# A last output quarter copied by two engines with one store moved to GpSimd, and V scaled first in four retention steps

## The chip, the cores and the metric

The kernel runs on one core of a Trainium2 chip. The metric is the time of one execution on the device in microseconds (us); where several runs are given, the median counts. The core's engines are TensorE (PE, matrix products; PEld is its loading of weights), VectorE (DVE), ScalarE (ACT), GpSimd (POOL) and SyncE (SP). Each runs its own list of instructions in order and waits on semaphores for what others produce. SyncE, ScalarE and GpSimd can issue DMA transfers; an engine that issues one is occupied while it does so.

## The reference

Retention (an attention without softmax, with a decay per head) over 8 sequences of 576 tokens, 8 heads of 64, followed by a two-layer network with hard-swish:

```python
scores = scale * np.matmul(q, k.transpose(0, 1, 3, 2))
gamma = 1.0 - 2.0 ** (-5.0 - np.arange(H, dtype=np.float32))
rel = pos[:, None] - pos[None, :]
Dmat = np.where(rel >= 0, gamma[:, None, None] ** rel[None, :, :], 0.0)
x = np.matmul(scores * Dmat, v)          # then heads side by side: 4608 x 512
h = x @ w_in                             # 512 -> 2048
g = h * np.clip(h + 3.0, 0.0, 6.0) / 6.0
out = g @ w_out                          # 2048 -> 512, float32
```

## The kernel before, in words

The tokens are cut into 36 pieces of 128: four from each sequence (pieces 0 to 3 are sequence 0, pieces 4 to 7 are sequence 1, and so on), and four "rest" pieces that hold the last 64 tokens of two sequences each. Four pieces make a block of 512 tokens; there are nine blocks, 0 to 8, the last one made of the rest pieces.

The decay factors: K stays plain, Q is scaled by gamma to one power and V by gamma to another (`scale_v`, L242, one VectorE multiplication per piece, in place). What is left of the decay is a 0/1 mask on the scores, applied by VectorE as it moves them from PSUM (`at`, L347), and a factor on the running state. A piece's output is the product of masked scores with scaled V (`intra`, L367) plus, where there is an earlier piece of the sequence, the product of the state with Q (L884 in these steps). The state takes up K times scaled V (`update_mm`, L383) and is then added and scaled by VectorE (`update_state`, L400, into `ta` and `ts`).

Two products per block follow: the first (L577) with 16 units of four matmuls, each finished by ScalarE (L585) and VectorE (L586); the second by plain matmuls for blocks 0 and 1 (L635), and for blocks 2 to 8 by seven products of half-size quarters in place of eight (`g2_seven`, L691, matmuls at L720), whose quarters C11, C12, C21 and C22 are put together by additions and stored. A list of steps by unit number (`put`, L979) sets by hand where the retention work of later pieces stands between the matmuls. The order in which instructions are written is the order on each engine; work in the list `later` is written when `run_later` is called.

`first_step(c)` (L862) is called for c = 3 to 8, between the units of block 0's second product and, for c = 8, in block 1's first. For c = 5 to 8 it ends piece c-1 (its `intra`, its `update_mm`, its state), and for c = 4 to 7 it begins piece c: scores, mask, and, as the last thing of the step, `scale_v(c)`. It also brings Q and K of piece c+1 into the layout that TensorE wants. So VectorE's order in a step is: state of c-1, mask of c, scaled V of c; and `intra(c)` in the following step needs both of the last two. K, Q and V of a piece come by GpSimd's DMAs (L103), three per piece.

For the last block the seven products end with the quarter C21. Its two halves lie in two PSUM banks, `xo` and `xtu`; each is copied to SBUF and stored as soon as its eight matmuls are done (`copy_half`, L749). Because the rest pieces belong to two sequences each, a store of the last block is two DMAs, the first issued by SyncE and the second by ScalarE (`store_quarter`, L678, for C11, C22 and C12; `store`, L617, for the halves of C21). C12 is the sum that VectorE makes last (L741, from `z`), shortly before the two halves of C21. The copies and sums take their SBUF tiles from one set of four (`osb`, `osh`).

Of the kernel before, what the change touches and what calls it, by code (L numbers as in the profile page):

```python
# [17 lines left out]
def kernel(  # L18
# [16 lines left out]
    nc = tc.nc  # L35
# [49 lines left out]
    def bank(shape, dtype, name):  # L85
        return psum.tile(shape, dtype, tag="ph", bufs=4, name=name)

    def bank_or(tag, shape, dtype, name):
        return psum.tile(shape, dtype, tag=tag, name=name) if tag else bank(shape, dtype, name)

    loaded = {}
    EARLY = 4
# [149 lines left out]
    def scale_v(c):  # L242
        vs = loaded[c]["qv"][:, 1]
        st.setdefault(c, {})["vs"] = vs
        nc.vector.tensor_tensor(out=vs, in0=vs, in1=gqv[:, 1], op=ALU.mult)
# [371 lines left out]
    def store(kb, mc, cols, src):  # L617
        if kb < B:
            r0 = kb * S + P * mc
            nc.sync.dma_start(out[r0:r0 + P, cols], src)  # L620
        else:
            for i in range(2):
                r0 = (2 * mc + i) * S + MAIN
                queue = nc.scalar if i else nc.sync
                queue.dma_start(out[r0:r0 + HALF, cols], src[i * HALF:i * HALF + HALF])
# [33 lines left out]
    def token_sums(kb, which, c0=0, c1=KH):  # L659

        gt = gts[kb]

        def a(i, j):
            return gt[:, KH * j + c0:KH * j + c1, TH * i:TH * i + TH]

        def s(name):
            if (kb, name) not in sums:
                sums[kb, name] = work.tile([P, KH, TH], FP16, tag=f"sum_{name}", bufs=1,
                                           name=f"sum_{name}_{kb}")
            return sums[kb, name]  # L670

        x, y, op = {"s1": (lambda: a(1, 0), lambda: a(1, 1), ALU.add),
                    "s2": (lambda: s("s1")[:, c0:c1], lambda: a(0, 0), ALU.subtract),
                    "s3": (lambda: a(0, 0), lambda: a(1, 0), ALU.subtract),
                    "s4": (lambda: a(0, 1), lambda: s("s2")[:, c0:c1], ALU.subtract)}[which]
        nc.vector.tensor_tensor(out=s(which)[:, c0:c1], in0=x(), in1=y(), op=op)  # L676

    def store_quarter(kb, i, j, src):  # L678

        cols = slice(NH * j, NH * j + NH)  # L680
        if kb < B:
            r0 = kb * S + TH * i
            nc.sync.dma_start(out[r0:r0 + TH, cols].rearrange("(u p) n -> p u n", u=2), src)
        else:
            rest = out.rearrange("(m x s) n -> x s m n", x=2, s=S)
            for x in range(2):
                queue = nc.scalar if x else nc.sync
                queue.dma_start(rest[x, MAIN:S, 2 * i:2 * i + 2, cols],
                                src[x * HALF:x * HALF + HALF])

    def g2_seven(kb, last=False):  # L691

        gt = gts[kb]

        def w(i, j):
            return wout16[:, KH * i:KH * i + KH, NH * j:NH * j + NH]

        def a(i, j):
            return gt[:, KH * j:KH * j + KH, TH * i:TH * i + TH]

        def s(name):
            return sums[kb, name]

        acc = {}

        def get(name):
            if name not in acc:
                if last and name == "x":
                    acc[name] = [psum.tile([P, NH], FP32, tag=t, name=f"x{t}_{kb}")
                                 for t in ("o", "tu")]  # L710
                else:
                    whole = bank([P, 2, NH], FP32, name=f"{name}_{kb}")
                    acc[name] = [whole[:, 0], whole[:, 1]]
                    wholes[name] = whole
            return acc[name]

        def product(name, u, left, right, first):
            dst = get(name)[u]
            for c in range(KH):
                newest[0] = nc.tensor.matmul(  # L720
                    dst, left()[:, c, P * u:P * u + P], right[:, c, :],
                    start=(first and c == 0 and (u == 0 or name not in wholes)),
                    stop=(c == KH - 1), skip_group_check=True)

        kept, wholes = {}, {}

        def parts(name, tile):
            if name in wholes:
                return [(wholes[name], tile)]
            return [(acc[name][u], tile[:, u]) for u in range(2)]  # L730

        def keep(name):
            kept[name] = work.tile([P, 2, NH], FP32, tag="keep_" + {"m5": "m1"}.get(name, name), bufs=1,
                                   name=f"keep_{name}_{kb}")
            for src, dst in parts({"m5": "z"}.get(name, "x"), kept[name]):
                nc.scalar.copy(dst, src)

        def total(i, j, name, src):
            osb = work.tile([P, 2, NH], FP32, tag="osb", bufs=4, name=f"osb_{kb}_{i}_{j}")
            for (a0, dst), (_, a1) in zip(parts(src, osb), parts(src, kept[name])):  # L740
                nc.vector.tensor_tensor(out=dst, in0=a0, in1=a1, op=ALU.add)  # L741
            store_quarter(kb, i, j, osb)

        def copy_total():
            osb = work.tile([P, 2, NH], FP32, tag="osb", bufs=4, name=f"osb_{kb}_1_0")
            nc.scalar.copy(osb, wholes["x"])
            store_quarter(kb, 1, 0, osb)

        def copy_half(u):  # L749
            osb = work.tile([P, NH], FP32, tag="osb", bufs=4, name=f"osh_{kb}_{u}")  # L750
            nc.scalar.copy(osb, acc["x"][u])
            store(kb, 2 + u, slice(0, NH), osb)

        def unit(name, u, left, right, first, then=()):
            def do():
                product(name, u, left, right, first)
                for f in then:
                    f()
            return do

        plan = [
            ("x", lambda: a(0, 0), w(0, 0), True, [lambda: keep("m1")]),
            ("y", lambda: a(0, 1), w(1, 0), True,
             [lambda: total(0, 0, "m1", "y"), lambda: token_sums(kb, "s3")]),
            ("x", lambda: s("s2"), wts["t2"], False, [lambda: keep("u2")]),
            ("z", lambda: s("s1"), wts["t1"], True,
             [lambda: keep("m5"), lambda: token_sums(kb, "s4")]),
            ("x", lambda: s("s3"), wts["t3"], False, [lambda: total(1, 1, "m5", "x")]),
            ("z", lambda: s("s4"), w(1, 1), False, [lambda: total(0, 1, "u2", "z")]),
            ("x", lambda: a(1, 1), wts["t4"], False, [] if last else [copy_total]),  # L770
        ]
        units = []
        for n, (name, left, right, first, then) in enumerate(plan):
            for u in range(2):
                after = then if u else []
                if last and n == len(plan) - 1:
                    after = [lambda u=u: copy_half(u)]
                units.append(unit(name, u, left, right, first, after))
        return units
# [82 lines left out]
    def first_step(c):  # L862


        old, new, b = c - 1 >= EARLY, c + 1 < 8, pieces[c - 1][1]
        if old:
            before = state_of.get(b)
            o = bank_or(None if c == 6 else "o", [P, NPAIR, P], FP32, name=f"o_{c - 1}")
            st[c - 1].update(o=o, first=True)
            copy = intra(c - 1, copy_later=True, more=before is not None)  # L870
            added = update_mm([c - 1])
            load_until(min(c + 5, 11))
            if c + 5 in (10, 11):
                hold(c + 5, added)
            update_state(c - 1, copies_later=True)
        if new:
            q_by_pe(c + 1)
        if old and new:
            run_later(9)
        if EARLY <= c < 8:  # L880
            scores(c, 0)
        if old and before is not None:
            for p in range(NPAIR):
                nc.tensor.matmul(o[:, p, :], tbd[before][:, p, :], st[c - 1]["qk"][:, 0, p, :],  # L884
                                 start=False, stop=(p == NPAIR - 1), skip_group_check=True)
        if new:
            k_by_pe(c + 1, None if old else "tu")
        if old:
            copy()
        if c < 8:  # L890
            run_later(9)
        if EARLY <= c < 8:
            scale_v(c)

    def transpose_q_and_load(c):

# [205 lines left out]
```

## Time and profile before

| | us |
|---|---|
| median of 3 runs | 294.66 |
| lowest, highest | 294.29, 294.87 |
| the profiled execution's own time | 294.43 |
| its span in the profile | 292.6 |
| busy: PE, DVE, ACT, POOL | 281.1, 227.6, 169.1, 104.3 |

The span runs from the first to the last instruction that the profile shows; the execution's own time lies 1.8 us above it. All times in rows are counted from the start of the span. A timeline row gives start, duration, engine, source line, operation, destination and sources with their shapes, and in brackets the idle time before it and what ended that. A "q" behind an engine's name marks its instruction queue: DMA issues and semaphore waits. In the chain of work that ended last, a row is start, duration, and the engine, tile and line that held the chain; "issue" is time in which an engine waited for nothing that the profile shows. A wait row reads: who waited for whom, us in total, times, longest.

### The profile page before, as it was taken

Reading aid. Unit: us, or ns where it says so; the run is one execution under the profiler, and the core shown is the slowest. Engines: PE = TensorE matmul, PEld = TensorE weight load, DVE = VectorE, ACT = ScalarE, POOL = GpSimd, SP = SyncE. Lnnn points to the kernel's source line nnn. Section 1 sums busy time; section 2 is a strip of 40 time slices with the busy share of each in tenths; the row PEclk is TensorE's granted clock in tenths of the full one; section 3 lists DMA queues with packets and bytes.
Section 4 is the critical chain, followed back from the end, with each engine's and each line's share of the span. In section 5 each row is a group of like instructions: output and inputs, shape, how many; then the busy total and the mean of one; then the engine's idle time right before and its main releaser. Section 6 shows DMA issues by size and latency. Waiting matters only on the chain.

```text
span 292.6 us, 8351 instructions
## 1 busy us (share of the span) xinstructions
PE 281.1 (96%) x3492; PEld 174.7 (60%) x3492; DVE 227.6 (78%) x377; ACT 169.1 (58%) x301; POOL 104.3 (36%) x130
## 2 busy tenths in 40 slices
PE   7699999999989999999999999999999999999993
PEld 2454445544544587458745874587458745874682
DVE  4858656798758997899789988998899588728860
ACT  6668537784357744774486448644864286338711
POOL 8753578159523432443234324455550000000000
PEclk9999999999999999999999999999999999999999
DMA  9999999999999989997999799979992240120014
GB/s 137 177 205 203 191 157 215 165 126 137 132 215 166 160 85 120 168 141 81 121 163 143 77 127 170 136 82 123 160 139 47 74 110 0 38 81 30 0 39 109
DMA packets 156631, 36.21 MB, mean 124 GB/s; under 512 B 143792, under 2 KB 155568, under 8 KB 156592
## 3 DMA queue, kind: packets, MB, share of 16 engines
q0 software_dynamic: 113104, 17.83, 89.3%
q1 hardware_dynamic: 42896, 17.31, 30.5%
q8 instruction: 27, 0.44, 0.7%
q10 hardware_dynamic: 592, 0.52, 0.5%
q14 instruction: 12, 0.10, 0.1%
HBM read 36.70 MB, written 9.44 MB: 158 GB/s over the span
## 4 chain that ended last, share of the span: by engine, by line
PE 91%; DMA 4%; POOL 2%; DVE 1%; issue 1%; ACT 0%; ACTq 0%; POOLq 0%
PE ph L577 41%; PE x L720 14%; PE pout L635 9%; PE z L720 8%; PE y L720 5%; DMA kn<-in_k_dram 3%; PE o L483 3%; PE sc L450 2%; PE o L504 1%; PE u L535 1%; PE ph L600 1%; POOL kn L103 1%; DMA out_dram<-osb 1%; PE xtu L720 1%; PE xo L720 1%
## 5 line engine op out<-in xcount | busy, mean ns | idle before, releaser
L577 PE MATMUL ph<-xt,win 128*128 128x512 f16 x560 | 122.3, 379 | 0.0
L586 DVE SCALAR_TENSOR_TENSOR gt<-u,ph 128x512 f16<-128x512 f32 x144 | 95.7, 685 | 22.6 <-ACT u L585 21.4
L585 ACT ACTIVATE u<-ph,cb 128x512 f32<-128x512 f32 x144 | 98.4, 688 | 25.7 <-PE ph L577 25.1
L577 PEld LDWEIGHTS <-win 128*128 128x128 f16 x560 | 54.7, 98 | 64.4
L103 POOL DMA_DIRECT2D kn<-in_k_dram x40 | 34.0, 850 | 40.7 <-PE ph L577 15.4
L103 POOL DMA_DIRECT2D qv<-in_v_dram x40 | 33.8, 846 | 38.8 <-PE ph L577 16.2
L720 PEld LDWEIGHTS <-sum_s 128*128 128x128 f16 x448 | 42.7, 98 | 5.3
L103 POOL DMA_DIRECT2D qv<-in_q_dram x36 | 30.2, 839 | 28.7 <-PE z L720 10.4
L720 PEld LDWEIGHTS <-gt 128*128 128x128 f16 x336 | 32.1, 98 | 5.5
L635 PE MATMUL pout<-wout,gt 128*128 128x512 f16 x128 | 29.6, 379 | 0.1
L720 PE MATMUL x<-wsum_t,sum_s 128*128 128x256 f16 x192 | 22.9, 273 | 0.0
L556 ACT CAST tm<-th 128x256 f16<-128x256 f32 x24 | 9.7, 405 | 20.3 <-DVE th L551 20.1
L635 PEld LDWEIGHTS <-gt 128*128 128x128 f16 x128 | 11.9, 98 | 13.2 <-issue 0.4
L456 DVE TENSOR_TENSOR at<-sc,mask 128x1024 f16<-128x1024 f32 x14 | 17.0, 1217 | 1.9 <-PE sc L450 1.9
L676 DVE TENSOR_TENSOR sum_s<-gt 128x1024 f16<-128x1024 f16 (+1 forms) x21 | 18.1, 864 | 0.2
L332 DVE TENSOR_TENSOR qv<-qv,gqv 128x1024 f16<-128x1024 f16 x26 | 17.8, 684 | 0.0
L514 ACT CAST xt<-o 128x512 f16<-128x512 f32 x28 | 15.0, 585 | 4.6 <-PE o L504 4.6
L567 DVE TENSOR_TENSOR ta<-u,th 128x256 f32<-128x256 f32 x24 | 10.2, 424 | 6.3 <-ACT th L554 5.2
L720 PE MATMUL z<-wout,sum_s 128*128 128x256 f16 x112 | 14.5, 274 | 0.0
L720 PE MATMUL y<-wout,gt 128*128 128x256 f16 x112 | 14.3, 273 | 0.0
L720 PE MATMUL z<-wsum_t,sum_s 128*128 128x256 f16 x112 | 13.6, 273 | 0.0
L720 PE MATMUL x<-wout,gt 128*128 128x256 f16 x96 | 11.5, 272 | 0.0
(118 smaller groups left out, 255.3 us busy)
## 6 DMA issues: line engine op xcount, KB each, us to landing
out_dram<-osb SPq DMA_DIRECT2D x32, 256.0 KB, 3.2
kn<-in_k_dram POOLq DMA_DIRECT2D x32, 128.0 KB, 5.9
qv<-in_v_dram POOLq DMA_DIRECT2D x32, 128.0 KB, 6.0
qv<-in_q_dram POOLq DMA_DIRECT2D x28, 128.0 KB, 5.9
wout<-in_moe_w_out_dram POOLq DMA_DIRECT2D x4, 512.0 KB, 15.2
win<-in_moe_w_in_dram POOLq DMA_DIRECT2D x3, 512.0 KB, 12.3
qf<-in_q_dram SPq DMA_DIRECT2D x4, 256.0 KB, 4.6
win<-in_moe_w_in_dram POOLq DMA_DIRECT2D x2, 256.0 KB, 8.3
```

The costliest lines, as they stand in the source:

```text
L103: loaded[c]["dma"].append(nc.gpsimd.dma_start(dst[p0:p0 + n], src[b, :, s0:s0 + n, :].rearrange("h s d -> s h d")))
L332: scaled = nc.vector.tensor_tensor(out=qv, in0=qv, in1=gqv, op=ALU.mult)
L456: nc.vector.tensor_tensor(out=at.rearrange("t a j p s -> t (a j p) s"), in0=sc.rearrange("t a j p s -> t (a j p) s"), in1=mask64[:, None, ...
L514: nc.scalar.copy(xt_at(cs[0], 0, 2 * P).rearrange("e p (j x s) -> e p j x s", j=2, x=2) [:, :, :, half, :], o[half].rearrange("e j p s -> ...
L556: nc.scalar.copy(tm, ta)
L567: nc.vector.tensor_tensor(out=ta, in0=st[c]["u"][1], in1=st[c]["sum"], op=ALU.add)
L577: newest[0] = nc.tensor.matmul(ph, win16[:, dmc, P * fc:P * fc + P], xt_of(kb)[:, dmc, :], start=(dmc == 0), stop=(dmc == NCC - 1))
L585: nc.scalar.activation(u, ph, ACTF.Relu, bias=cb[:, 0:1], scale=1.0 / 6.0)
L586: nc.vector.scalar_tensor_tensor(out=gts[kb][:, fc, :], in0=u, scalar=1.0, in1=ph, op0=ALU.min, op1=ALU.mult)
L635: nc.tensor.matmul(pout, gt[:, fc, P * mc:P * mc + P], wout16[:, fc, :], start=(fc == 0), stop=(fc == NFC - 1))
L676: nc.vector.tensor_tensor(out=s(which)[:, c0:c1], in0=x(), in1=y(), op=op)
L720: newest[0] = nc.tensor.matmul(dst, left()[:, c, P * u:P * u + P], right[:, c, :], start=(first and c == 0 and (u == 0 or name not in whol ...
```

## The change

Three edits. In `copy_half` the second half of the last quarter (u = 1, `xtu`) is copied by VectorE; the first stays with ScalarE. In `store_quarter`, for the last block, the second DMA of a quarter with j > i is issued by GpSimd; of the three quarters that are stored there only C12 (i = 0, j = 1) is meant. In `first_step`, `scale_v(c)` for c = 4 to 7 stands at the beginning of the step, in front of the state of piece c-1 and of the mask, and no longer at its end.

```diff
@@ store_quarter
             for x in range(2):
-                queue = nc.scalar if x else nc.sync
+                queue = (nc.gpsimd if j > i else nc.scalar) if x else nc.sync
                 queue.dma_start(rest[x, MAIN:S, 2 * i:2 * i + 2, cols],
                                 src[x * HALF:x * HALF + HALF])
@@ copy_half
-            nc.scalar.copy(osb, acc["x"][u])
+            if u:
+                nc.vector.tensor_copy(osb, acc["x"][u])
+            else:
+                nc.scalar.copy(osb, acc["x"][u])
             store(kb, 2 + u, slice(0, NH), osb)
@@ first_step
         old, new, b = c - 1 >= EARLY, c + 1 < 8, pieces[c - 1][1]
+        if EARLY <= c < 8:
+            scale_v(c)
         if old:
...
         if c < 8:
             run_later(9)
-        if EARLY <= c < 8:
-            scale_v(c)
```

## The prediction

> **What bounds the kernel now.** I read the page first, then the chain of work that ended last, then waits and timeline of the two places that the change touches.
>
> ```profile
> span 292.6 us, 8351 instructions
> ...
> PE 91%; DMA 4%; POOL 2%; DVE 1%; issue 1%; ACT 0%; ACTq 0%; POOLq 0%
> ```
>
> The chain is TensorE for 91% of the span. A change on another engine moves the end only where the chain leaves PE. It does so in two stretches that the change touches: once while block 0's output product runs, and after the last matmul. The first, from the chain:
>
> ```profile
> 48.72 0.99 issue
> 49.72 0.43 DVE qv L245
> 50.14 0.04 issue
> 50.19 0.41 PE o L372 x8
> ```
> ```profile
> PE o L372 <- DVE qv L245: 0.5, 1, 0.5
> ```
>
> The product of the masked scores of piece 6 with its scaled V (L372) starts at 50.19, 0.04 us after VectorE has scaled that V (L245). The second row is the waits view of that stretch: it is the only wait of PE's matmuls there, 0.5 us. The other three steps wait for their V on the weight side only, while matmuls issued earlier still run.
>
> The second place is the tail, rows of several engines from the timeline:
>
> ```profile
> 283.18 1.04 PE L720 MATMUL xtu<-wsum_t,sum_s 128*128 128x256 f16 x8
> 284.25 0.42 DVE L741 TENSOR_TENSOR osb<-xtu,keep_m 128x256 f32<-128x256 f32 x1 [0.39 <-PE xtu L720]
> ...
> 285.80 1.04 PE L720 MATMUL xo<-wsum_t,gt 128*128 128x256 f16 x8
> 286.00 0.69 DVE L741 TENSOR_TENSOR osb<-z,keep_u 128x512 f32<-128x512 f32 x1 [1.32 <-PE z L720]
> 286.67 1.04 PE L720 MATMUL xtu<-wsum_t,gt 128*128 128x256 f16 x8
> ...
> 286.72 0.63 ACTq L688 DMA_DIRECT2D out_dram<-osb  x1
> 287.45 0.37 ACT L751 COPY osh<-xo 128x256 f32<-128x256 f32 x1 [4.30 <-DMA out_dram<-osb]
> 287.86 0.51 ACTq L625 DMA_DIRECT2D out_dram<-osh  x1
> 288.49 0.37 ACT L751 COPY osh<-xtu 128x256 f32<-128x256 f32 x1 [0.66 <-ACT osh L751]
> 288.89 0.51 ACTq L625 DMA_DIRECT2D out_dram<-osh  x1
> ```
>
> Here ScalarE does everything in series. It issues C12's second store (0.63 us), copies the first half of the last quarter, issues its store (0.51 us), copies the second half, issues that. xo is whole at 285.80 + 1.04 = 286.84 and its copy starts at 287.45; xtu is whole at 287.71 and its copy starts at 288.49. So 0.78 us of the way from the last matmul to the last store is ScalarE being busy.
>
> The end hangs on that store, by these rows: its landing, the landing of C12's stores, and what the closing waits on SyncE's queue waited for.
>
> ```profile
> DMA to landing us min/median/max: 2.0/2.1/2.2
> ...
> DMA to landing us min/median/max: 2.5/2.7/2.9
> ...
> SPq L1097 <- DMA out_dram<-osh: 1.3, 2, 0.7
> ```
>
> The last pair is issued at 288.89 and lands by 288.89 + 2.2 = 291.1; the remaining 1.5 us up to 292.6 are the closing waits and barrier, which stay.
>
> **The change part by part: the tail.** Without C12's second store in front of it, ScalarE copies xo when PE has ended it. DVE followed PE by 284.25 - (283.18 + 1.04) = 0.03 us; I take the same for ScalarE. Copy at 286.87 to 287.24, its stores issued to 287.79 on both queues; SyncE's queue has only C12's first store in front, issued like ScalarE's at 286.72. VectorE ends C12's sum at 286.69 and is idle after it, so it copies xtu from 287.71 + 0.03 = 287.74. A plain PSUM copy of this shape does not occur on VectorE. The add of the same shape took 0.42 us (284.25), ScalarE's copy 0.37; it might cost less than either, and the floor is nothing at all, since PE ends at 287.71. I take 0.42 as the nearest row of the same engine. The copy ends at 288.16 and the two stores are issued at 288.19, against 288.89: a gain of 0.70 us, with a copy of half the time 0.91.
>
> What takes the cover away is GpSimd's store. Its price is not in the trace, since GpSimd issues loads only; the nearest are the 64-partition loads of the rest pieces:
>
> ```profile
> L103 POOL DMA_DIRECT2D qv<-in_v_dram x8: 679/679/687, 195.4 to 217.2; - x8
> ...
> DMA to landing us min/median/max: 2.5/3.6/5.3
> ...
> 61.01 0.69 DVE L332 TENSOR_TENSOR qv<-qv,gqv 128x1024 f16<-128x1024 f16 x1
> ...
> 61.99 0.88 POOL L103 DMA_DIRECT2D kn<-in_k_dram  x1 [9.36 <-DVE qv L332]
> ```
>
> GpSimd starts 61.99 - 61.70 = 0.29 us after VectorE releases it, so its store starts at 286.69 + 0.29 = 286.98. With 2.5 us it lands at 289.5, with 3.6 at 290.6, with 5.3 at 292.3. The new last stores land at 288.19 + 2.2 = 290.4. I take 3.3, between the 2.9 of C12's slower store as it is now and the loads' 3.6, which ran beside other traffic: 290.3, just covered. Beyond 3.4 us GpSimd's store sets the end; a quicker one gains nothing more, because the others still land at 290.4. The page DMA: Bandwidth & Descriptors of the Trainium skill, section Latency and other measured facts, speaks against this move: first byte about 1 us on GpSimd's path against about 0.6 us on that of SyncE and ScalarE. An estimate by that page adds 0.4 us to the 2.9 us, so 290.28, and the sum would stay as it is; no run here shows the difference yet.
>
> **V of pieces 4 to 7.** Removed: nothing; four scalings of 0.42 us move ahead of the state in their step. VectorE's rows:
>
> ```profile
> 39.46 1.22 DVE L655 TENSOR_TENSOR wsum_t<-wout 128x2048 f16<-128x2048 f16 x1
> ...
> 43.32 0.42 DVE L245 TENSOR_TENSOR qv<-qv,gqv 128x512 f16<-128x512 f16 x1
> ...
> 46.40 0.41 DVE L245 TENSOR_TENSOR qv<-qv,gqv 128x512 f16<-128x512 f16 x1
> ...
> 48.58 1.22 DVE L347 TENSOR_TENSOR at<-sc,mask_wide 128x1024 f16<-128x1024 f32 x1
> 49.72 0.41 DVE L245 TENSOR_TENSOR qv<-qv,gqv 128x512 f16<-128x512 f16 x1
> 50.77 0.42 DVE L411 TENSOR_TENSOR ta<-u,ts 128x256 f32<-128x256 f32 x1 [0.64 <-PE u L394]
> ```
>
> The scaling keeps its place behind the mask in time, but is now that of the next piece: 5 at 43.32, 6 at 46.40, 7 at 49.72, and 4 at about 40.7, behind the weight sum (39.46). L372 then waits for the mask alone, which ends at 48.58 + 1.22 = 49.80. With the same 0.05 us from VectorE's end to the matmul it starts at 49.85 in place of 50.19: a gain of 0.34 us. What is late next is that mask, so the 0.5 cannot be had whole. The state's add (50.77, idle 0.64 before it) comes at about 50.43 and finds VectorE free at 50.14, so the moved scaling costs it nothing.
>
> Queued behind a scaling that has to wait for its V would be state, mask and through them PE. The loads:
>
> ```profile
> 18.35 0.88 POOL L103 DMA_DIRECT2D qv<-in_v_dram  x1 [1.05 <-DMA win<-in_moe_w_in_dram]
> ...
> DMA to landing us min/median/max: 2.5/5.1/16.1
> ...
> L103 POOL DMA_DIRECT2D qv<-in_v_dram x1: 876/876/876, 30.9 to 30.9; - x1
> ...
> DMA to landing us min/median/max: 10.2/10.2/10.2
> ...
> L103 POOL DMA_DIRECT2D qv<-in_v_dram x1: 896/896/896, 33.5 to 33.5; - x1
> ...
> L103 POOL DMA_DIRECT2D qv<-in_v_dram x1: 876/876/876, 39.4 to 39.4; - x1
> ...
> DMA to landing us min/median/max: 6.6/6.6/6.6
> ```
>
> V of piece 4 is issued at 18.35 and, with the worst landing of all loads (16.1), there by 34.5, wanted at 40.7. V 5 lands at 30.9 + 10.2 = 41.1, wanted at 43.3; V 6, with the same 10.2, at 43.7, wanted at 46.4; V 7 at 39.4 + 6.6 = 46.0, wanted at 49.7. Margins of 2.2 us and more. L372 now has two VectorE results to wait for at different places; if that adds a wait of its own to PE's stream, I bound it by the 0.04 us "issue" steps of the chain, for four steps 0.16, nothing where PE waits anyway.
>
> Sum: 0.70 + 0.34 = 1.04 us from the profiled execution's 294.43, so 293.39; that execution lies 0.23 under the median of 294.66, and against the median it is 293.62.
>
> **The rivals.** First, GpSimd's store ends last and the kernel is slower. It is the one price without a row of its own. From 291.1 - 286.98 = 4.1 us on the tail gains nothing, from 5.05 on it outweighs the V part and 0.59 us more; at the loads' 5.3 the end moves by 292.28 - 291.1 = +1.18, less 0.34, to 295.50. For it: loads in the same form did take that long, and GpSimd has been idle since 217. Against: the quiet ones took 2.5. In between, at 4.1, the tail is a draw and the time 294.32.
>
> Second, the V gain is lost further on, because something that does not follow PE holds it:
>
> ```profile
> 83.22 0.94 issue
> ...
> PE o L504 <- issue: 0.9, 1, 0.9
> ...
> q8 instruction: 27, 0.44, 0.7%
> ```
>
> In the middle of a group of matmuls PE stands 0.94 us for nothing that the profile names. If that is an instruction block arriving at its own time, PE comes 0.34 earlier and waits 0.34 longer; the time is then 294.66 - 0.70 = 293.96. The page Runtime: NRT & Kernel Launch of the Trainium skill, section Instruction fetch mechanics, says each engine's sequencer fetches its next 16 KiB block while it executes; the queue's row, 0.44 MB in 27, agrees with that size. Against the rival: a fetch asked for by PE's own progress moves along with it, and in the waits view from 54 us on this one row is all that PE's matmuls wait for.
>
> Third, the copy of xo at 287.45 was not held by the store's issue but, as its row says, by a landing. Then moving the store does not free it: its issue ends at 288.37, ScalarE's half of the last store goes out at 288.41, a gain of 0.48, and the time is 293.84. Against it: the issue ends at 286.72 + 0.63 = 287.35, 0.10 before the copy, and between the next issue's end (288.37) and the next copy (288.49) there is the same 0.12; and the buffer it takes is the fourth of four (L750), whose last store was block 7's, issued before block 8's first product.
>
> **How the numbers follow.** Both parts as summed: 0.52, 293.6, its own range 293.2 to 294.0. Copy held by a landing: 0.08. V gain lost: 0.15. GpSimd's store late, the tail a draw: 0.13. GpSimd's store later, slower: 0.12. The low end takes the cheap copy (0.91), the whole 0.5 at the V wait and 0.18 for the spread of the runs, 294.29 to 294.87: 293.1. The high end holds the draw and half of that spread above it, 294.7, and leaves out the slower case. 0.2%, 0.59 us, is about what a measurement of this kernel can tell from no change. Under 294.07 lie most of the first three cases, 0.66; above 295.25 two thirds of the last, 0.08; the rest, 0.26, is no change.
>
> **What would show it.** Right: L372 of piece 6 starts 0.05 behind the mask and not behind L245, at 49.85; no VectorE idle time before L245 put down to a load; xo's copy at 286.87 less the 0.34; the gap from the last matmul's end to the last store's issue 0.48 in place of 1.18. Wrong: a closing wait on SyncE put down to GpSimd's store; a stall near 83 longer by 0.34; the scaling of V waiting for its load.

## The result, and the profile after

| | before | changed |
|---|---|---|
| median of 21 runs each (us) | 294.87 | 293.65 |
| lowest, highest | 293.02, 296.57 | 292.63, 294.69 |
| profiled execution: time, span | 294.43, 292.6 | 293.9, 292.1 |
| last matmul's end to the end of the span | 4.93 | 4.44 |

The ratio is 0.996 with a 95% interval of 0.9945 to 0.9976: faster, by 0.24% to 0.55%, 0.7 to 1.6 us. The same pair on another chip (experiment 9) gave 0.9969, 0.9942 to 0.9995. The forecast was 293.6, 0.35% under the 294.66 of the runs shown then. Single executions spread over 2 to 3.5 us, which is more than the whole effect, so what follows leans on distances inside the traces.

The changed kernel's page, and its chain where block 0's output product runs (start, duration, what held the chain):

```profile
span 292.1 us, 8352 instructions
...
PE 93%; DMA 2%; POOL 1%; DVE 1%; issue 1%; POOLq 0%
```
```profile
48.96 1.15 DVE at L347
50.11 0.04 issue
50.15 0.41 PE o L372 x8
```

The link between VectorE and PE is now the mask, not the scaled V; the 0.99 of "issue" and the 0.43 of L245 behind the mask are gone from the chain. VectorE's rows there:

```profile
48.88 1.22 DVE L347 TENSOR_TENSOR at<-sc,mask_wide 128x1024 f16<-128x1024 f32 x1
50.02 0.41 DVE L245 TENSOR_TENSOR qv<-qv,gqv 128x512 f16<-128x512 f16 x1
50.73 0.42 DVE L411 TENSOR_TENSOR ta<-u,ts 128x256 f32<-128x256 f32 x1 [0.30 <-PE u L394]
```

The scaling at 50.02 is piece 7's. The mask ends at 48.88 + 1.22 = 50.10 and the product starts at 50.15. The state's add finds VectorE free and waits for PE, as before.

The tail, rows of five engines from the timeline, then the landing of the last pair of stores, that of C12's two (SyncE's first, GpSimd's second), and the closing wait:

```profile
286.62 1.04 PE L720 MATMUL xtu<-wsum_t,gt 128*128 128x256 f16 x8
...
286.82 0.37 ACT L754 COPY osh<-xo 128x256 f32<-128x256 f32 x1 [3.73 <-PE xo L720]
287.22 0.52 ACTq L625 DMA_DIRECT2D out_dram<-osh  x1
...
286.94 0.62 POOL L688 DMA_DIRECT2D out_dram<-osb  x1 [69.10 <-DVE osb L741]
...
287.69 0.42 DVE L752 COPY osh<-xtu 128x256 f32<-128x256 f32 x1 [1.06 <-PE xtu L720]
...
288.15 0.51 ACTq L625 DMA_DIRECT2D out_dram<-osh  x1
```
```profile
DMA to landing us min/median/max: 2.2/2.3/2.4
...
DMA to landing us min/median/max: 2.5/2.7/2.9
...
SPq L1100 <- DMA out_dram<-osb: 0.9, 1, 0.9
```

The last store goes out 288.15 - 287.66 = 0.49 us behind the last matmul, where it was 1.18. GpSimd's store lands at 286.94 + 2.9 = 289.8, the last pair by 288.15 + 2.4 = 290.6. The closing wait names GpSimd's store because SyncE asks for that semaphore second in its list; the last landing comes 0.7 us later. That last landing is SyncE's half of the last pair. Its row and its landing, before and then changed:

```profile
288.88 0.49 SPq L625 DMA_DIRECT2D out_dram<-osh  x1
...
DMA to landing us min/median/max: 2.0/2.0/2.0
```
```profile
288.14 0.68 SPq L625 DMA_DIRECT2D out_dram<-osh  x1
...
DMA to landing us min/median/max: 2.4/2.4/2.4
```

ScalarE's half landed 2.2 us after its issue in both.

The span is only 0.5 us shorter, because two other places moved. PE's first product of block 0 starts at 18.47 in place of 18.17, and the stall near 83 us is longer:

```profile
82.86 0.09 PE o L504 x10
82.95 1.14 issue
84.10 0.38 PE o L504 x22
```

It took 0.94 before. The following table takes the start out. It is worked out from the traces: the start of the first L577 matmul; counted from there, the start of L372 for piece 6 and the end of the last matmul; PE's stalls that the chain shows as "issue" between 74 and 90 us; and the tail from the last matmul's end to the end of the span.

| kernel | first L577 | L372, piece 6 | stalls | last matmul's end | tail |
|---|---|---|---|---|---|
| before | 18.17 | 32.02 | 0.08, 0.94 | 269.55 | 4.93 |
| changed | 18.47 | 31.69 | 1.14 | 269.19 | 4.44 |
| 9: changed again | 18.43 | 31.67 | 0.66 | 268.68 | 4.45 |
| 1: tail alone | 17.81 | 32.02 | 1.22 | 269.59 | 4.45 |
| 2: V alone | 18.78 | 31.69 | 0.60 | 268.64 | 4.94 |
| 4: without GpSimd's store | 17.86 | 31.69 | 0.95 | 269.00 | 4.59 |
| 6: last store by GpSimd | 18.17 | 31.69 | 0.35, 0.94 | 269.49 | 4.88 |
| 7: GpSimd's store, no VectorE copy | 19.00 | 31.69 | 0.31, 1.21 | 269.74 | 4.53 |
| 3: changed, 64 instructions in front | 18.26 | 31.68 | none | 267.88 | 4.46 |
| 10: the same again | 18.07 | 31.69 | none | 268.09 | 4.47 |
| 11: before, 64 in front | 18.63 | 32.01 | none | 268.53 | 4.94 |
| 8: 64 in front, half masks | 19.26 | 31.47 | none | 268.04 | 4.47 |
| 5: changed, 240 in front | 22.41 | 31.68 | 1.54 | 269.58 | 4.48 |

### The profile page after: what moved, and what is told of

Same layout as the page of the kernel before. It is cut to its first block, busy times and chain, and to the rows that moved or that the text cites. A ratio compares the mean times of both kernels' runs of the same rounds, so it can differ in the third digit from the quotient of the medians.

```text
span 292.1 us, 8352 instructions
## 1 busy us (share of the span) xinstructions
PE 281.8 (96%) x3492; PEld 175.4 (60%) x3492; DVE 227.9 (78%) x378; ACT 168.6 (58%) x300; POOL 104.9 (36%) x131
## 4 chain that ended last, share of the span: by engine, by line
PE 93%; DMA 2%; POOL 1%; DVE 1%; issue 1%; POOLq 0%
PE ph L577 41%; PE x L720 14%; PE pout L635 9%; PE z L720 9%; PE y L720 5%; PE o L483 3%; DMA kn<-in_k_dram 2%; PE sc L450 2%; PE o L504 1%; PE u L535 1%; PE ph L600 1%; PE xtu L720 1%; PE xo L720 1%; PE o L372 1%; PE trk L256 1%; POOL kn L103 1%
## 5 line engine op out<-in xcount | busy, mean ns | idle before, releaser
L577 PE MATMUL ph<-xt,win 128*128 128x512 f16 x560 | 122.3, 379 | 0.0
L577 PEld LDWEIGHTS <-win 128*128 128x128 f16 x560 | 54.6, 98 | 64.5
L688 POOL DMA_DIRECT2D out_dram<-osb x1 | 0.6, 620 | 69.1 <-DVE osb L741 69.1
```

Of the source, the lines that this page charges most:

```text
L577: newest[0] = nc.tensor.matmul(ph, win16[:, dmc, P * fc:P * fc + P], xt_of(kb)[:, dmc, :], start=(dmc == 0), stop=(dmc == NCC - 1))
```

## The experiments

**1. The tail alone.** `first_step` as before.

```diff
-        if EARLY <= c < 8:
-            scale_v(c)
         if old:
...
         if c < 8:
             run_later(9)
+        if EARLY <= c < 8:
+            scale_v(c)
```

> The tail's two edits alone; V is scaled at the end of the step as before. Theory A (both parts carry through to the end): the last matmul's end to the end of the span falls from 4.89 us (before) to about 4.44 (the changed kernel's), intra of piece 6 (L372) waits for L245 and starts 0.05 us behind it, about 1.47 us behind the state's matmuls' last wait as before; the time is 0.45 us under before, a ratio of 0.9985. Theory B (the V part is swallowed at the stall near 83 us): the same trace, but the time equals that of the changed kernel, a ratio of about 0.996.

Measured: tail 4.45, L372 back at 32.02, stall 1.22; 294.02 against 294.40, ratio 0.9993 (0.9973 to 1.0013). Both theories have this trace, so only the time can choose: its interval holds A's 0.9985, and B's 0.996 lies just under it. (The 4.89 us expected for the kernel before goes by the rounded span; the table has 4.93.)

**2. V alone.** The tail's two edits undone.

```diff
-                queue = (nc.gpsimd if j > i else nc.scalar) if x else nc.sync
+                queue = nc.scalar if x else nc.sync
...
-            if u:
-                nc.vector.tensor_copy(osb, acc["x"][u])
-            else:
-                nc.scalar.copy(osb, acc["x"][u])
+            nc.scalar.copy(osb, acc["x"][u])
```

> The moved scaling of V alone; the tail as before. Theory A: L372 of piece 6 starts 0.05 us behind the end of its mask, 0.34 us earlier against the matmuls in front of it, and the last matmul ends 0.34 us earlier than before's against the same start: ratio 0.9988. Theory B: PE comes to the stall at its 1729th instruction 0.34 us earlier and leaves it at the same distance from the preceding block boundary, so the stall is about 1.2 us in place of 0.94 and the ratio is 1.000. The tail takes 4.89 us in both.

Measured: L372 at 31.69, tail 4.94, ratio 0.998 (0.9953 to 1.0007), an interval that holds A's 0.9988 and B's 1.000. In the trace the stall was 0.60, not theory B's 1.2, so in this execution PE kept its lead and more. The chain of this kernel at the second boundary:

```profile
83.19 0.09 PE o L504 x10
83.27 0.60 issue
83.87 0.38 PE o L504 x22
```

B's fixed distance from the boundary before is refuted (6.95 us here, 7.29 in the kernel before); the stall's length varies from run to run.

**3. Shifting PE's program by 64 instructions.** 32 products of 8 columns in front of the warm-up, where PE waits for its first data anyway.

```diff
-    def warm(n, cols):
+    def warm(n, cols, more=0):
...
+        for _ in range(more):
+            nc.tensor.matmul(w[:, 0:8], zeros[:, 0:P], zeros[:, 0:8], start=True, stop=True)
...
-    warm(7, MBLK)
+    warm(7, MBLK, 32)
```

> The changed kernel with 32 tiny matmuls (8 columns, onto zeros, in the bank of the first warm-up, 64 PE instructions) put in front of the warm-up, while PE waits for its first data. Theory B (the stall is a block of 256 instructions that arrives 7.3 to 7.5 us after PE crossed the boundary before): boundaries fall 64 instructions earlier in the program, the two dense blocks then take 7.5 us each to run, so the stall near 83 us goes from 1.1 to under 0.2 us and the time falls by 0.9 to 1.1 us against the changed kernel, to about 292.6. Theory C (the stall belongs to the place in the program, a wait that the profile does not name): it stays at the 11th matmul of L504, 1.1 us, and the time stays at 293.7.

Measured: 292.74 against 294.40, ratio 0.9952 (0.9926 to 0.9977). This kernel's chain runs through the same place (L504 is L506 here) without a gap:

```profile
82.27 0.38 PE sc L452 x32
82.64 0.27 PE o L506 x32
82.91 1.83 PE pout L637 x8
```

The place in the program needs no wait; theory C falls. The state of the start is not why the stall is gone: kernels 8 and 11, with the same 64 instructions and a granted clock of 0.91 over the first 18 us like the changed kernel's, have no such stall.

**4. Without GpSimd's store.** ScalarE issues C12's second store again; VectorE's copy and the V part stay.

```diff
-                queue = (nc.gpsimd if j > i else nc.scalar) if x else nc.sync
+                queue = nc.scalar if x else nc.sync
```

> The changed kernel with C12's second store issued by ScalarE again: VectorE's copy and the V part stay. Theory A: xo's copy starts behind the issue, 0.58 us later than in the changed kernel against the last matmul; xtu's copy by VectorE stays where it is, but its second store is issued behind xo's, 0.26 us later (0.75 behind the last matmul's end in place of 0.48), and the tail is 4.7 us in place of 4.44. Theory D (GpSimd's store, landing 2.9 us after its issue, holds up the others): the last stores land faster than 2.2 to 2.4 us after their issue, and the tail is 4.45 or shorter, so that GpSimd's part of the change is worth nothing.

Measured: tail 4.59, ratio 0.9978 (0.9957 to 1.0). The end of this kernel's chain on PE, then ScalarE's rows of its timeline:

```profile
285.99 0.89 PE xtu L720 x8
```
```profile
286.60 0.37 ACT L754 COPY osh<-xo 128x256 f32<-128x256 f32 x1 [4.31 <-DMA out_dram<-osb]
...
287.62 0.80 ACTq L625 DMA_DIRECT2D out_dram<-osh  x1
```

PE ends at 286.86, so the last store goes out 0.76 behind it (0.75 expected). But the tail is only 0.15 longer than the changed kernel's, not 0.27, and lies between the two theories: GpSimd's store is worth about half of what the issue times say.

**5. A shift of 240 instructions** (`warm(7, MBLK, 120)`).

> The changed kernel with 120 tiny matmuls (8 columns, 240 PE instructions) in front of the warm-up. Theory B (a block of 256 instructions arrives 7.3 to 7.5 us after PE crossed the boundary before): two successive blocks hold the two dense stretches, and without a stall PE would run them in 5.2 and 4.5 us. So PE stands 2.1 us or more at the first of the two boundaries, near 77 us, and 0.5 to 2.8 at the second, near 85; the time rises by 1.5 to 3.8 us against the changed kernel, to 295.2 to 297.5. Theory C (place in the program): one stall of about 1.2 us at the 11th matmul of L504, the time of the changed kernel.

Measured: 299.59 against 294.30. A large part of it is an effect that was not meant. The 120 products delay the transposes whose end releases the third and fourth load of Q (`load_q`), and the first L577 starts 3.9 us later. The stalls came out only in part as expected: none at the first of the two boundaries, which PE now crosses at 82.25 and where 2.1 or more was expected, and 1.54 at the second, within 0.5 to 2.8. This kernel's chain there:

```profile
86.80 0.15 PE o L506 x18
86.95 1.54 issue
88.49 0.31 PE o L506 x14
```

It stands behind the 18th matmul of its group, 8 matmuls further on, where with 240 in front the boundary is 16 instructions later in the program. So the stall follows the boundary and not the place; but the time that a block takes to arrive is no constant 7.3.

**6. The last store by GpSimd too.**

```diff
-                queue = nc.scalar if i else nc.sync
+                queue = (nc.gpsimd if mc == 3 else nc.scalar) if i else nc.sync
```

> The changed kernel with the second store of the last half, the one that ends the kernel, issued by GpSimd as well. GpSimd starts 0.26 us behind VectorE and its store landed 2.7 to 2.9 us after its issue, so this one is issued 0.70 us behind the last matmul's end and lands at 3.4 to 3.6 in place of 2.9: the tail goes from 4.44 to between 4.95 and 5.15 us. If GpSimd's store cost what the slow loads cost (the prediction's 5.3 us), it would land at 6.0 and the tail would be 7.5.

Measured: tail 4.88, a little under the range; one execution, 294.31. GpSimd's last row in this kernel's timeline, and the landing of the last pair of stores:

```profile
288.41 0.55 POOL L625 DMA_DIRECT2D out_dram<-osh  x1 [0.85 <-DVE osh L752]
```
```profile
DMA to landing us min/median/max: 2.3/2.3/2.4
```

Last in the queue and with 64 KB, GpSimd's store lands 2.3 us after its issue, no slower than SyncE's. It starts 0.26 us later than ScalarE's did, but the last landing of all comes only 0.12 later against the last matmul. The other 0.32 of the tail's 0.44 lie behind that landing: SyncE's closing waits ask for GpSimd's semaphore first here, so eight waits on other semaphores, about 0.06 us each, are passed only after it; in the changed kernel three are. The prediction's 5.3 us is far from both this and the 2.9 of C12's.

**7. GpSimd's store without VectorE's copy.** `copy_half` as before.

> The changed kernel with both halves of the last quarter copied by ScalarE; C12's second store stays with GpSimd. Theory A' (the two edits of the tail remove the same wait): ScalarE copies xo at once, issues its store until 0.1 us behind the last matmul's end, copies xtu from 0.13 to 0.50 and its last store goes out at 0.54, against 0.49 in the changed kernel: the tail is 4.5 us. Theory A'' (the edits add up, 0.34 for the copy and 0.15 for the store as the run without GpSimd's store splits them): the tail is 4.78.

Measured: tail 4.53; one execution, 295.08, its first L577 at 19.00. The last matmul ends at 288.74 here; ScalarE's last two rows in the timeline:

```profile
289.00 0.37 ACT L751 COPY osh<-xtu 128x256 f32<-128x256 f32 x1 [0.72 <-PE xtu L720]
289.40 0.51 ACTq L625 DMA_DIRECT2D out_dram<-osh  x1
```

Theory A' holds: the copy starts 0.26 behind PE (0.13 expected) and the store goes out at 0.66 (0.54 expected). Each edit of the tail alone takes most of the gain (0.40 and 0.34 of 0.49), since both remove the same thing, ScalarE's being busy when xtu is ready.

**8. Half masks for piece 6**, with the 64 instructions in front.

```diff
+        if c == 6:
+            def halves():
+                for p0 in (0, 2):
+                    nc.vector.tensor_tensor(
+                        out=at[:, :, p0:p0 + 2, :], in0=sc[:, :, p0:p0 + 2, :],
+                        in1=mask01[:, None, None, :].to_broadcast([P, 2, 2, P]), op=ALU.mult)
+            later.append(halves)
+            return
```

> The changed kernel with the 64 instructions in front of the warm-up, and with the mask of piece 6 applied in two halves of 512 columns. The first half is ready 0.55 us sooner, so the first product of piece 6 with V no longer waits: PE's 0.22 us there goes to 0.05 or less, the second half comes just in time. Against the run with the 64 instructions alone 0.15 to 0.2 us less: ratio to before 0.9945, near 292.6 where before is 294.4. If the halves cost more than they bring (two VectorE instructions of 0.65 in place of one of 1.22), the state of piece 6 is later but waits for PE anyway, and the time stays.

Measured: 293.41 against 294.30, ratio 0.9971 (0.9946 to 0.9996); a miss. L372 starts 0.21 earlier, without a wait, but its eight matmuls then take 0.58 us in place of 0.41, waiting for the second half, and the next step's L372 is only 0.05 earlier. Counted from L577 the last matmul ends at 268.04, between the 267.88 and 268.09 of the two runs with the 64 instructions alone, so the halves neither bring nor cost anything that the traces show; this kernel's first L577 is the latest but that of kernel 5. PE's rows of this kernel's timeline (L372 is L382 here):

```profile
49.77 1.03 PE L645 MATMUL pout<-wout,gt 128*128 128x512 f16 x4
50.73 0.58 PE L382 MATMUL o<-at,qv 128*64 128x128 f16 x8
```

**9 to 11. The changed kernel again, with the 64 instructions, and before with them**, side by side.

> The changed kernel once more, on the same chip as the two runs beside it. Ratio to before 0.996 to 0.9975 (0.34 us from the V part, 0.45 from the tail, 0.24 from the small stall that before has near 77 us, jitter of the stall near 83 of 0.3 either way); the stall at the 1729th instruction of PE 0.6 to 1.4 us.

> The changed kernel with the 64 instructions in front of the warm-up, once more: no stall near 83 us, and 0.8 to 1.2 us less than the changed kernel beside it, so a ratio to before of 0.9925 to 0.9945. If the first run's gain was the state of the first 18 us alone (its granted clock there was 1.00, that of the changed kernel 0.91), the ratio is that of the changed kernel beside it.

> The kernel before with the 64 instructions in front of the warm-up, none of the change. If the V part carries through to the end, then without the stall the changed kernel's matmuls end 0.34 us sooner than this one's, counted from the first product of block 0 (L577), and its tail is 0.45 shorter: this one lies 0.8 us above the changed kernel with the same 64 instructions and 1.0 to 1.2 under before, a ratio to before of 0.996. If the V part were lost elsewhere, the difference would be 0.45.

Measured against a before of 294.57: 293.88, ratio 0.9969 (0.9942 to 0.9995); 292.93, ratio 0.9939 (0.9918 to 0.996); 294.04, ratio 0.9975 (0.9948 to 1.0003). The first two are as expected. Kernel 11 lies only 0.53 us under before, where 1.0 to 1.2 was expected, though its interval holds the expected 0.996. One reason is in its chain: with the stall gone, PE meets a wait that the profile does name.

```profile
75.40 7.95 DMA qk<-qv
83.35 0.04 issue
83.39 0.32 PE sc L452 x16
```

The transposed Q of a piece arrives at 83.35, 8 us after its transfer began, where PE was ready at 83.0. Without the stall this is the next bound, 0.3 us behind. Between 11 and the two runs with the change, the last matmul's end counted from L577 differs by 0.65 and 0.44 us, for which 0.34 was expected. At PE's 1473rd instruction kernel 11 is 0.32 and 0.33 behind them, which is the V part whole. Behind it that wait adds about 0.35, and kernel 10 loses about 0.2 at a later boundary, the 2241st instruction. The changed kernel with 64 instructions in front is the fastest of all kernels run, at 292.74 and 292.93.

## Why the prediction was right, point by point

- **V part, 0.34 us: right, mechanism and size.** L372 of piece 6 starts 0.05 behind the mask. In every kernel with the moved scaling and whole masks it is at 31.67 to 31.69, in every one without at 32.01 to 32.02. No V was late, and the other steps did not move: no price of a second wait on PE was seen.
- **V gain lost at the stall near 83 us (0.15): not so, as far as the noise lets one see.** Eight traces have PE's instructions as they were. Counted from L577, PE crosses the 1473rd instruction at 58.12 to 58.14 us in the six with the V part and at 58.46 in the two without, once what PE stands at that crossing itself is taken off (0.24 in the kernel before, 0.51 and 0.47 in kernels 6 and 7, by the starts of the matmuls). From there to the 1729th it takes 6.95 to 7.57 us with the V part, 7.27 on average, and 7.29 and 7.58 without; the rival wants 0.34 more with it. From there to the last matmul's end it is 203.55 to 203.57 in all eight. So the lead is carried through, but a jitter of 0.3 either way, as large as the lead, lies on top of it. In the one profiled pair the later start (0.30) took back nearly all of it; the 0.21 more at this stall is made up by the 0.24 that the kernel before stands at the 1473rd.
- **Tail, 0.70 us: mechanism right, size off; the term is the landing of the last stores.** The copies began and the last stores were issued where the sum had them (VectorE's copy 0.42 us, last issue 0.69 earlier). But the sum carried over the landing, 2.2 us. ScalarE's half still lands in 2.2, but SyncE's, which had landed in 2.0, now takes 2.4 and comes last; its issue took 0.68 in place of 0.49. So the tail fell by 0.49. In SyncE's queue the last store now stands 0.79 us behind the one before it, in place of 1.03. In experiment 7, which has GpSimd's store too, it stands 0.96 behind and lands in 2.0, so GpSimd's store alone is not the reason. That the closeness of the stores is the reason is argued from these three distances; no run varied it alone.
- **GpSimd's store, taken as 3.3 us: 2.9, so it never set the end.** In every trace that has it, it landed 2.7 to 2.9 us after its issue, so the rival on the slower side falls. The estimate from the Trainium skill, DMA: Bandwidth & Descriptors, section Latency and other measured facts (0.4 us more to the first byte on GpSimd's path), is not borne out as a later landing: 2.9 for GpSimd's half against 2.9 for ScalarE's of the same size before.
- **Copy held by a landing (0.08): wrong.** Without the issue in front xo's copy starts when PE is done, and in experiment 4, with the issue back, again 0.58 us later, though its row still names a landing.
- **The signs of being wrong.** Two of the three showed up and did not mean what they were put down for. The closing wait does name GpSimd's store, but that store lands 0.7 us before the last one. The stall is longer in the profiled pair, by 0.20, and in kernel 7, by 0.27, but not in the other four with the V part (0.60 to 0.95, against 0.94 in the kernel before). No scaling of V in the four steps waited for its load.
- **The sum.** 0.34 + 0.49 = 0.83 us, 0.28%, lies inside the interval. The measured median differs by 1.22; the rest is the spread of the start and of the stall, and is not given to either part. That the measured 0.40% lies closer to the forecast's 0.35% than to this sum is luck: the forecast had 0.21 us more in the tail than the traces show. One end of the forecast's range is mis-added: 294.32 and half of the spread of 0.58 make 294.6, not 294.7; nothing hangs on it.

## What to carry to other kernels

Two edits that free the same engine at the same moment do not add up: price them together, and try each alone. When an issue moves earlier, carry the landing as a term of its own: here it grew by 0.2 us where the stores came closer together. In a program of many small matmuls, find out whether an unexplained PE gap sits at a fixed count of instructions. Here a shift of the program by 64 of them, on top of the change, was worth about as much as the change itself (0.95 us from kernel 9 to kernel 10; the change 1.22 in the result and 0.69 in experiment 9). On the kernel before alone it was 0.53, which is not clear of the noise.

## What the runs showed of the hardware

The "issue" gap near 83 us fits the arrival of a block of PE's instructions. In before and in every kernel with the same PE instructions it stands behind the 1729th in the trace, 256 behind the 1473rd, and PE resumes 1.3 to 1.5 us after the end of a transfer on q8, the queue that the profile calls "instruction"; each of its 27 transfers is one packet of 16 KiB. From the traces' packets and instruction counts (us); PE crosses a count when the next matmul behind it starts:

| kernel | PE crosses the 1473rd | transfer begins | transfer ends | PE resumes behind the 1729th |
|---|---|---|---|---|
| before | 76.87 | 81.84 | 82.77 | 84.16 |
| changed | 76.60 | 81.68 | 82.63 | 84.10 |
| 1 | 76.28 | 81.49 | 82.44 | 83.86 |
| 2 | 76.92 | 81.62 | 82.56 | 83.87 |
| 4 | 76.00 | 80.95 | 81.97 | 83.31 |
| 6 | 76.81 | 81.73 | 82.67 | 84.10 |
| 7 | 77.61 | 82.85 | 83.78 | 85.17 |
| 9 | 76.54 | 81.15 | 82.10 | 83.56 |

The transfer begins 4.6 to 5.2 us after PE crosses the 1473rd. PE runs these 256 instructions, many of them matmuls of 64 x 64, in 6.2 us, less than the 7.0 to 7.6 until it can go on. With a shift of 64 each of the two blocks takes 7.5 us to run, and the gap is gone.

Two things stay open. What delays the transfer was not tried, and the load of the DMA engines alone does not explain it. In the kernel before, the DMA share of the windows view (packets that overlap count each) is 1.8 to 2.0 from 76.9 to 81.8, while PE's next transfer has not begun. Behind the crossing at 73.02 it is 2.3, and the next transfer begins after 0.5 us; behind that at 106.09 it is 1.8, and the next begins after 0.7. And at the 1473rd itself PE stands 0.08, 0.35 and 0.31 us in kernels before, 6 and 7, where the last transfer on q8 had ended 1.7, 2.8 and 2.7 us before PE went on, so its end is not the whole account. The Trainium skill, Runtime: NRT & Kernel Launch, section Instruction fetch mechanics, has blocks of 256 instructions, which the counts confirm, and calls the crossing "mostly hidden"; at this boundary it cost 0.6 to 1.5 us.

The start is as uneven: the first L577 begins between 17.81 and 19.26 us in kernels that differ in nothing before it but the 64 tiny products. It goes with the clock that TensorE was granted over the first 18 us: at 1.00 (before, 1, 3, 4, 6, 10) it begins at 17.81 to 18.26, at 0.91 or 0.81 (changed, 2, 7, 8, 9, 11) at 18.43 to 19.26. Kernels 4 and 6, with the change's V part, are among the first six and kernel 11, without any of the change, among the others, so the 0.30 us between the starts of the profiled pair (1.00 before, 0.91 changed) is not put down to the change.
